# A fused attention and feed-forward kernel: the splits of the next v are placed in other slots of the seven-product tiles

## The chip, the cores and the metric

The kernel runs on one core of a Trainium2 chip. The metric is the device time of one execution, in microseconds (us), as the median of a few runs; three runs of the kernel before gave 2086.27, 2087.79 and 2088.13 us.

## The reference

Channel attention over 4 batches, and a feed-forward layer on its output, both in float32:

```python
def _attn_ref(q, k, v, tau):                       # q, k, v: (4, 6080, 256)
    qn = q / (np.linalg.norm(q, axis=1, keepdims=True) + 1e-06)
    kn = k / (np.linalg.norm(k, axis=1, keepdims=True) + 1e-06)
    s = kn.transpose(0, 2, 1) @ qn / tau           # 256 x 256 for each batch
    s = s - s.max(-1, keepdims=True)
    a = np.exp(s)
    a /= a.sum(-1, keepdims=True) + 1e-09
    return (v @ a).astype(np.float32)

def _moe_ref(x, w_in, w_out):                      # x: (24320, 256), w_in: (256, 2048), w_out: (2048, 256)
    h = x @ w_in
    g = np.maximum(0.01 * h, h)
    return (g @ w_out).astype(np.float32)
```

## The kernel before, in words

The kernel multiplies the attention matrix of a batch into `w_in`, so that a tile of v goes straight to h. A batch has 6 tiles of v, of twice 512 columns (the last two: twice 496), 24 tiles in all, counted here from 0 to 23. A tile is worked through in 8 **periods** (p0 to p7); each makes four 128-row blocks of h from seven block products (Strassen's scheme in Winograd's form: `block_product`, L1069, three matmuls each, since every operand is split into a high and a low half), applies the leaky unit, splits the result again and multiplies it with `w_out`.

In tiles 18 to 22 (`FAST`, the **seven-product tiles**) the product with `w_out` is also done with seven products instead of eight. They are called P1 to P7 (`fast_out`, L1206) and are issued one to four periods after the operand was made. A period of such a tile has 7 block products and 6 products with `w_out`: 13 times 3, so 39 matmuls. The seventh one, P4, of all 8 periods of a tile is put at the end of the next tile's p3 (`last_outs`): 24 matmuls, of which 13 are issued at the end of p3 and 11 in p4. So p3 has 52 matmuls and p4 has 50; these are the two long periods.

`fast_slot` (L1275) writes out one such period; each engine's instructions stand in the order in which it is called. TensorE's x and z are PSUM banks with one buffer each. In the order of VectorE (DVE) a period is:

- the middle slot, `slot("dve", ...)`, which takes work of the queue `dve` as long as its planned length (us) fits into the room given for this period;
- a slot for `dve_end`, then the low halves of C12 and C11 (`low`, L1167, the two `g_pair<-g_b`);
- the **first add** `add(i, h22, z)` (L1106): it reads bank z, and the block product "B22" that writes to z again (`block_product(i, p, z, S4, "B22", ...)`) waits for it;
- the low halves of T1 and T3, the second add `add(i, h12, z)`, the low halves of T2 and T4;
- a slot for `dve_end`, the low half of C22 (`g_pair<-g_a`), and in p3 and p4 a slot `dve` at the period's end.

The queue `dve` holds the work for the **next** tile's v. It is filled at given periods (`at(w + n, ...)`), where w is p0 of the tile. First come four maxima of v (`v_seen`, L158), then the gathering of the maximum over partitions (`gather` and `spread`, L163 to L177), the factors (`v_found`: L191 to L204 and L973), and 18 steps of `v_parts`: seven operands are split, each with a high half (`v_split_of`, L1012) and a low half (L1015), and four differences are made in place in `v_raw` (L1036). The tile `v_raw` has one buffer: the load of the v after the next (`v_load`, L996, two DMAs of 512 KB each on SyncE's queue) waits until the last split has read it. It is issued with p7 in the program:

```python
            at(w - (i in FAST) if i else 3, v_load, i + 1)
            elif i in FAST:
                at(w, v_scale_work, i + 1)
                for n in range(6):
                    at(w + 2 + n, v_go, i + 1, (3, 5, 5, 2, 2, 2)[n])
```

The queue `dve_end` takes the products P1 to P7 out of PSUM when a tile's last matmul of each was issued (`fast_end`): L1228 combines a bank and an earlier result, L1233 two results. The products with `w_out` of the last tile (23, with eight products, `ffn_out`, L1385) need the four banks `ps_o` that P1 to P4 of tile 22 leave.

On the POOL queue, each period issues four DMAs that add one g into another (`summed`, L1174); T1 to T4 are made from these sums.

Of the kernel before, what the change touches and what calls it, by code (L numbers as in the profile page):

```python
# [39 lines left out]
def channel_attention_ffn(  # L40
# [1095 lines left out]
    def p_has(g):  # L1136
        return g // NPAIR in FAST
# [137 lines left out]
    def fast_slot(i, p):  # L1275

        g = i * NPAIR + p
        n = widths[i % NT]
        seeded = not (p == 0 and widths[i % NT] > widths[(i - 1) % NT])
        w_split.pop((i, p - 1) if p else (i - 1, NPAIR - 1), None)  # L1280
        sums_start(g)
        order = ("P5", "P7", "P6", "P1", "P3") if p == 3 else ("P5", "P7", "P1", "P3", "P6")
        fast_outs(g, *order[:4 if p == 4 else 5])
        x, z = bank("x"), bank("z")
        block_product(i, p, x, A11, "B11", True, False)
        if seeded:
            run("act", lambda: nc.scalar.copy(out=z[:, 0:n], in_=x[:, 0:n]))
        else:
            h11 = taken(i, x)
        if g - 1 in fast_h:  # L1290
            run("act", unit, i - (p == 0), (p - 1) % NPAIR, "C12", fast_h.pop(g - 1), True)
        out(6)
        fast_do("act", high, g - 4, "T4")
        slot("dve", (3.0, 1.5, 2.3, 2.8, 2.8, 1.3, 1.3, 1.3)[p])
        block_product(i, p, z, A12, "B21", not seeded, True)
        block_product(i, p, x, S2, "T2", False, False)
        if not seeded:
            add(i, h11, z)
        run("act", unit, i, p, "C11", z if seeded else h11)
        h12 = taken(i, x)  # L1300
        out(4)
        slot("dve_end", 1.5)
        fast_do("act", high, g - 1, "C12")
        run("act", high, i, p, "C11")
        fast_do("act", high, g - 2, "T1")
        fast_do("dve", low, g - 1, "C12")
        run("dve", low, i, p, "C11")
        fast_outs(g, "P2", *(["P6"] if p == 4 else []))
        block_product(i, p, z, S1, "T1", True, False)
        block_product(i, p, x, S3, "T3", False, False)  # L1310
        h22 = taken(i, x)
        add(i, h22, z)
        out(6)
        fast_do("act", high, g - 2, "T3")
        fast_do("act", high, g - 3, "T2")
        slot("act_end", 0.65)
        fast_do("dve", low, g - 2, "T1")
        if p == 4:
            slot("dve_end", 0.8)
        fast_do("dve", low, g - 2, "T3")  # L1320
        if not p_has(g - 2):
            slot("dve", 1.5)
        block_product(i, p, x, A22, "T4", False, True)
        block_product(i, p, z, S4, "B22", False, True)
        run("act", unit, i, p, "C21", x, True)
        run("act", unit, i, p, "C22", h22)
        run("act", high, i, p, "C22")
        add(i, h12, z)
        fast_h[g] = h12
        last_outs(g)  # L1330
        out(15 if p == 3 else 24)
        if not p_has(g - 3):
            run("dve", low, i, p, "C22")
        fast_do("dve", low, g - 3, "T2")
        fast_do("dve", low, g - 4, "T4")
        slot("dve_end", 1.5)
        if p in (3, 4) or not p_has(g - 3):
            slot("dve", 1.3)
        if p_has(g - 3):
            run("dve", low, i, p, "C22")  # L1340

    def fast_rest(g):

# [80 lines left out]
    def slot(queue, room):  # L1424
        engine = queue.split("_")[0]
        while todo[queue] and todo[queue][0][0] <= room and todo[queue][0][1].ready():
            length, fn = todo[queue].popleft()
            room -= length
            with in_order(engine):
                ins = fn()  # L1430
            issued[engine] = ins
# [352 lines left out]
    for i in range(NTILES):  # L1784
        w = i * NPAIR
        if i + 1 < NTILES:
            at(w - (i in FAST) if i else 3, v_load, i + 1)
            if i + 1 < T16:
                at(w + (2 if i else 5), v_begin, i + 1)
                at(w + (4 if i else 6), v_work, i + 1, 2, 7)  # L1790
                at(w + 7, v_work, i + 1, 7, 11, i > 0)
            elif i in FAST:
                at(w, v_scale_work, i + 1)
                for n in range(6):
                    at(w + 2 + n, v_go, i + 1, (3, 5, 5, 2, 2, 2)[n])
            else:
                at(w + 1, v_scale_work, i + 1)
                at(w + 3, v_go, i + 1, 3)
                at(w + 4, v_go, i + 1, 3)
                at(w + 5, v_go, i + 1, 3)  # L1800
                at(w + 6, v_go, i + 1, 3)
        for p in range(NPAIR):
            if i:
                at(max(NPAIR - 2, w + p - 3), w_load, i, p)
# [233 lines left out]
    for i in range(NTILES):  # L2038
        for p in range(NPAIR):
            now[0] = i * NPAIR + p  # L2040
            for name in ("pe", "act"):
                todo[name].extend(todo[name + "_next"])
                todo[name + "_next"].clear()
            for fn, args in steps.get(i * NPAIR + p, ()):
                fn(*args)
            if i in FAST:
                assert (i // NT, p) in w_done 
                fast_slot(i, p)
                continue
            if i - 1 in FAST:  # L2050
                fast_rest(now[0])
            if p:
                w_split.pop((i, p - 1))
            x, y, z = bank("x"), bank("z" if i else "y"), bank("z")
            block_product(i, p, x, A11, "B11", True, False)
            h11 = taken(i, x)
            block_product(i, p, y, A12, "B21", True, True)
            slot("act", 0.65 if i else 0.75 if p else 1.5)
            slot("act_late", 0.65)
            add(i, h11, y)  # L2060
            if last is not None:
                leaky(i, p - 1, "C12", last)
                last = None
            slot("dve", 1.45 if i else 1.3)
            out(5)
            slot("pe", 1 if i and len(todo["pe"]) < 2 else 3)
            if i:
                leaky(i, p, "C11", h11)
            slot("dve", 2.2 if i else 2.6 if p < NPAIR - 1 else 1.5)
            if not todo["dve"]:  # L2070
                slot("dve_idle", 0.9)
            slot("act_end", 0.65)
            slot("dve_end", 1.5)
            assert (i // NT, p) in w_done
            block_product(i, p, x, S2, "T2", False, False)
            h12 = taken(i, x)
            if i == 0:
                leaky(i, p, "C11", h11)
                slot("dve", 1.0)
            if i:  # L2080
                slot("act", 1.8)
            block_product(i, p, z, S1, "T1", True, False)
            out(5)
            slot("pe", 1 if i or p else 2)
            block_product(i, p, x, S3, "T3", False, False)
            h22 = taken(i, x)
            add(i, h22, z)
            if i == 0:
                slot("act", 2.2)
            slot("dve", 1.45 if i else 2.8)  # L2090
            if not todo["dve"]:
                slot("dve_idle", 0.9)
            slot("act_end", 0.65)
            slot("dve_end", 1.5)
            out(8)
            slot("pe", 0 if i or p else 2)
            slot("pe_late", 1)
            if i == 0:
                slot("act", 0.6)
            else:  # L2100
                leaky(i, p, "C22", h22)
            block_product(i, p, x, A22, "T4", False, True)
            block_product(i, p, z, S4, "B22", False, True)
            add(i, h12, z)
            leaky(i, p, "C21", x)
            slot("act", 0.65 if i else 0.75)
            slot("act_late", 0.65)
            slot("dve", 0.8)
            if i == 0:
                leaky(i, p, "C22", h22)  # L2110
                slot("dve", 1.5)
            if i or p == NPAIR - 1:
                leaky(i, p, "C12", h12)
            else:
                last = h12
            out(24)
            last_outs(now[0])
            if i == NTILES - 1 and p < 4:
                outs.append(ffn_out(i, p, False))
                held.append(ffn_out(i, p, True))  # L2120
                if p == 3:
                    outs.extend(held)
                continue
            outs.append(ffn_out(i, p))
# [32 lines left out]
```

## Time and profile before

| | |
|---|---|
| median of three runs | 2087.79 us (2086.27 to 2088.13) |
| the profiled execution | 2087.2 us, its span 2085.2 us |
| TensorE (PE) busy | 2055.3 us, 99% of the span |
| VectorE (DVE) busy | 1691.6 us, 81% |
| ScalarE (ACT) busy | 1497.3 us, 72% |
| mean granted TensorE clock | 0.995 of full speed |
| tile 18, p0 to p7 | 1607.68 to 1675.03 us, 67.35 us |
| tile 19 | 1675.03 to 1747.93 us, 72.90 us |
| tile 20 | 1747.93 to 1828.97 us, 81.04 us |
| tile 21 | 1828.97 to 1908.48 us, 79.51 us |
| tile 22 | 1908.48 to 1987.50 us, 79.02 us |
| tile 23, to the end | 1987.50 to 2085.20 us, 97.70 us |

A period begins where TensorE starts its first matmul into bank x (`A11`); the times of the tiles are read from these. Times in all views are us from the span's start. In the timeline a row gives the start, the length, the engine, the line, the operation and its tiles; several like instructions in a row are one row (x2), and the idle time of the engine before the row stands in brackets with what ended it. An engine starts its next instruction before the one before has quite ended in these views, so the distance of two starts is what an instruction takes of the engine's time.

### The profile page before, as it was taken

The numbers are of one execution on the slowest core, as the hardware profiler recorded it, in microseconds if no ns is written. First come the engines' busy times: TensorE is split into PE (matmuls) and PEld (weight loads), VectorE is DVE, ScalarE is ACT, GpSimd is POOL, SyncE is SP. The second block draws the span as 40 slices with busy tenths as digits, with TensorE's granted clock in tenths as the row PEclk, the third lists the DMA queues.
The fourth block names the chain that finished last, engine by engine and source line by source line (L and its number), as shares of the span: only waits on it lengthen the run. The fifth ranks groups of instructions, "written<-read, shape, count | busy, mean of one in ns | idle before, by whom it ended". The sixth has DMA issues, their size and how long they took to land.

```text
span 2085.2 us, 27771 instructions
## 1 busy us (share of the span) xinstructions
PE 2055.3 (99%) x9516; PEld 1183.5 (57%) x9516; DVE 1691.6 (81%) x3112; ACT 1497.3 (72%) x2715; POOL 256.1 (12%) x331
## 2 busy tenths in 40 slices
PE   9999999999999999999999999999999999999998
PEld 8888888888865544544444444444444443434443
DVE  8988888878788878788888887877778897887873
ACT  6577777766578888877666666666666887877874
POOL 0000000000012232220001000000000343333310
PEclk9999999999999999999999999999999999999999
DMA  9946676655576997752333323332333776666630
GB/s 374 393 159 205 203 245 213 177 170 183 183 204 200 238 253 216 185 154 77 131 134 116 116 97 108 133 99 80 100 127 122 144 154 131 122 138 134 127 65 25
DMA packets 145438, 335.37 MB, mean 161 GB/s; under 512 B 18480, under 2 KB 38832, under 8 KB 145296
## 3 DMA queue, kind: packets, MB, share of 16 engines
q1 hardware_dynamic: 105776, 251.72, 36.0%
q0 software_dynamic: 39152, 81.55, 19.0%
q8 instruction: 75, 1.23, 0.3%
q14 instruction: 67, 0.55, 0.1%
q10 hardware_dynamic: 368, 0.32, 0.1%
HBM read 221.97 MB, written 57.42 MB: 134 GB/s over the span
## 4 chain that ended last, share of the span: by engine, by line
PE 91%; DVE 5%; ACT 2%; DMA 2%; issue 1%; SPq 0%; DVEq 0%; ACTq 0%
PE ps_o L1385 36%; PE ps_x L1069 22%; PE ps_z L1069 17%; PE ps_o L1206 5%; PE ps_s L336 4%; PE ps_o L336 2%; PE ps_y L336 2%; PE ps_s L1672 1%; PE ps_s L1206 1%; PE ps_y L1206 1%; DVE h L1106 1%; DVE g_pair L1167 1%; DMA v_raw<-in_vT_dram 1%; DVE v_split L1015 1%; ACT g L1089 0%
## 5 line engine op out<-in xcount | busy, mean ns | idle before, releaser
L1385 PE MATMUL ps_o<-g_split,w_out_split 128*128 128x512 f16 (+3 forms) x3456 | 846.5, 381 | 0.0
L1069 PE MATMUL ps_x<-v_split,w_split 128*128 128x512 f16 (+3 forms) x2280 | 621.7, 381 | 2.4 <-ACT h L1112 1.6
L1106 DVE TENSOR_TENSOR h<-ps_z,h 128x512 f32<-128x512 f32 (+1 forms) x529 | 360.6, 682 | 178.2 <-ACT h L1112 158.3
L1069 PEld LDWEIGHTS <-w_split 128*128 128x128 f16 x3024 | 293.7, 98 | 367.1 <-issue 34.7
L1099 DVE TENSOR_TENSOR g_split<-g,g_split 128x512 f16<-128x512 f32 (+3 forms) x576 | 393.6, 684 | 113.0 <-ACT g_split L1089 106.0
L1069 PE MATMUL ps_z<-v_split,w_split 128*128 128x512 f16 (+3 forms) x1704 | 463.5, 381 | 18.0 <-DVE h L1106 17.7
L1112 ACT COPY h<-ps_x 128x512 f32<-128x512 f32 (+1 forms) x537 | 309.3, 576 | 229.0 <-PE ps_x L1069 225.4
L1089 ACT ACTIVATE g<-h 128x512 f32<-128x512 f32 (+1 forms) x456 | 284.6, 624 | 202.9 <-DVE h L1106 200.4
L1385 PEld LDWEIGHTS <-w_out_split 128*128 128x128 f16 x2496 | 244.2, 98 | 291.6 <-issue 3.6
L1089 ACT ACTIVATE g_split<-h 128x512 f16<-128x512 f32 (+3 forms) x432 | 263.7, 610 | 0.0
L1385 PEld LDWEIGHTS ps_o<-g_split,w_out_split 128*128 128x128 f32 x1152 | 216.3, 188 | 43.5
L1069 PEld LDWEIGHTS ps_x<-v_split,w_split 128*128 128x128 f32 x576 | 107.7, 188 | 22.3 <-ACT g L1089 0.4
L1167 DVE TENSOR_TENSOR g_pair<-g_b,g_pair 128x512 f16<-128x512 f32 (+1 forms) x120 | 78.6, 682 | 32.2 <-ACT g_pair L1162 32.0
L1206 PE MATMUL ps_o<-g_pair,w_out_split 128*128 128x512 f16 (+1 forms) x360 | 100.5, 382 | 0.4 <-ACT g_pair L1162 0.3
L1015 DVE SCALAR_TENSOR_TENSOR v_split<-v_raw,v_scale,v_split 128x512 f16<-128x512 f32 (+1 forms) x125 | 93.0, 744 | 3.8
L1089 ACT ACTIVATE g<-ps_x 128x512 f32<-128x512 f32 (+1 forms) x152 | 89.5, 589 | 7.4 <-PE ps_x L1069 5.2
L1095 ACT CAST g_split<-g 128x512 f16<-128x512 f32 (+3 forms) x144 | 88.6, 615 | 4.6
L1069 PEld LDWEIGHTS ps_z<-v_split,w_split 128*128 128x128 f32 x408 | 76.2, 188 | 16.6 <-DVE h L1106 1.4
L1206 PEld LDWEIGHTS <-spare 128*128 128x128 f16 x480 | 47.6, 99 | 58.4 <-issue 4.2
L234 POOL MEMSET qk_raw<- 64x512 f32 x5 | 2.6, 521 | 585.2 <-ACT sq L260 267.6
L270 POOL DMA_DIRECT2D spare<-sq x48 | 43.9, 915 | 223.4 <-ACT sq L269 223.2
L1162 ACT CAST g_pair<-g_b 128x512 f16<-128x512 f32 (+1 forms) x120 | 69.7, 614 | 0.0
(263 smaller groups left out, 2353.0 us busy)
## 6 DMA issues: line engine op xcount, KB each, us to landing
w_split<-w_dram SPq DMA_DIRECT2D x104, 448.0 KB, 4.0
w_split<-w_dram SPq DMA_DIRECT2D x40, 896.0 KB, 5.0
qk_raw<-in_q_dram SPq DMA_DIRECT2D x115, 256.0 KB, 4.9
qk_raw<-in_k_dram SPq DMA_DIRECT2D x115, 256.0 KB, 5.1
v_raw<-in_vT_dram SPq DMA_DIRECT2D x32, 512.0 KB, 4.8
out_dram<-o_sb SPq DMA_DIRECT2D x64, 256.0 KB, 3.3
spare<-sq POOLq DMA_DIRECT2D x47, 256.0 KB, 5.3
g_a<-g_a POOLq DMA_DIRECT2D x32, 256.0 KB, 3.2
```

Of the source, the lines that this page charges most:

```text
L336: mm = nc.tensor.matmul(out=out, lhsT=lhsT, rhs=rhs, start=start, stop=stop, skip_group_check=True)
L1015: return nc.vector.scalar_tensor_tensor(out=sp[:, 1, 0:w], in0=src, scalar=up, in1=sp[:, 0, 0:w], op0=ALU.mult, op1=ALU.subtract)
L1069: mm = nc.tensor.matmul(out=ps[:, 0:n], lhsT=w[:, x, a, :], rhs=sp[:, y, 0:n], start=first and k == 0, stop=k == 2, skip_group_check=True,)
L1089: return nc.scalar.activation(out=to, in_=h[:, 0:n], func=AF.Prelu, alpha=0.01, scale=G_SCALE if i >= T16 else 1.0)
L1095: issued["act"] = nc.scalar.copy(out=sp[:, 0, 0:n], in_=out[:, 0:n])
L1099: issued["dve"] = nc.vector.tensor_tensor(out=sp[:, 1, 0:n], in0=out[:, 0:n], in1=f32(sp[:, 0, 0:n]), op=ALU.subtract)
L1106: issued["dve"] = nc.vector.tensor_tensor(out=h[:, 0:n], in0=ps[:, 0:n], in1=h[:, 0:n], op=ALU.add)
L1112: issued["act"] = nc.scalar.copy(out=h[:, 0:n], in_=ps[:, 0:n])
L1162: return nc.scalar.copy(out=sp[:, 0, 0:n], in_=g32[i, p, HELD.get(name, name)][:, 0:n])
L1167: return nc.vector.tensor_tensor(out=sp[:, 1, 0:n], in0=g32[i, p, HELD.get(name, name)][:, 0:n], in1=sp[:, 0, 0:n], op=ALU.subtract)
L1206: issued["pe"] = nc.tensor.matmul(out=ps[:, 0:n], lhsT=fast_lhsT(i, p, prod, x), rhs=sp[:, y, 0:n], start=p == 0 and k == 0, stop=p == NPA ...
L1385: issued["pe"] = nc.tensor.matmul(out=o_ps[i][j][h][:, 0:n], lhsT=wo_lhsT(i, x, f, h), rhs=sp[:, y, 0:n], start=p == 0 and early and k == ...
```

## The change

Four places. In `fast_slot` the rooms of the middle slot change for p1 (1.5 to 2.4), p3 and p4 (2.8 to 1.5). The `dve` slot at the period's end comes after the low half of C22 instead of ahead of it in p3 and p4, and has room 1.9 in p3 and in the first periods of tile 18, and 3.2 in p4. The steps of the next v are queued from p1 to p5 (1, 4, 6, 6, 2) instead of p2 to p7 (3, 5, 5, 2, 2, 2). In the last tile a slot of `dve_end` stands at the end of each period. The line numbers of the new file are one higher from L1332 on, and by up to three further down.

```diff
@@ -1291,7 +1291,7 @@
         fast_do("act", high, g - 4, "T4")
-        slot("dve", (3.0, 1.5, 2.3, 2.8, 2.8, 1.3, 1.3, 1.3)[p])
+        slot("dve", (3.0, 2.4, 2.3, 1.5, 1.5, 1.3, 1.3, 1.3)[p])
         block_product(i, p, z, A12, "B21", not seeded, True)
@@ -1329,15 +1329,16 @@
         out(15 if p == 3 else 24)
+        wide = p in (3, 4) or not p_has(g - 3)
         if not p_has(g - 3):
             run("dve", low, i, p, "C22")
         fast_do("dve", low, g - 3, "T2")
         fast_do("dve", low, g - 4, "T4")
         slot("dve_end", 1.5)
-        if p in (3, 4) or not p_has(g - 3):
-            slot("dve", 1.3)
         if p_has(g - 3):
             run("dve", low, i, p, "C22")
+        if wide:
+            slot("dve", 3.2 if p == 4 else 1.9)
@@ -1791,8 +1792,8 @@
                 at(w, v_scale_work, i + 1)
-                for n in range(6):
-                    at(w + 2 + n, v_go, i + 1, (3, 5, 5, 2, 2, 2)[n])
+                for n in range(5):
+                    at(w + 1 + n, v_go, i + 1, (1, 4, 6, 6, 2)[n])
@@ -2114,6 +2115,8 @@
             out(24)
+            if i == NTILES - 1:
+                slot("dve_end", 1.5)
             last_outs(now[0])
```

No instruction is added or dropped, and on PE, ACT, POOL and SP the instructions stand in the same order as before. Only DVE's order changes, in tiles 18 to 23. Three places of it:

DVE before, tile 19's last period and tile 20's first (in both, the two `g_pair<-g_b` are the low halves of C12 and C11, the row after them is the first add, and `v_split` and the maxima belong to the next tile's v):

```order
L1106 TENSOR_TENSOR h<-ps_z,h 128x512
L1167 TENSOR_TENSOR g_t<-g_b,g_t 128x512
L1167 TENSOR_TENSOR g_pair<-g_b,g_pair 128x512
L1167 TENSOR_TENSOR g_pair<-g_a,g_pair 128x512
L1015 SCALAR_TENSOR_TENSOR v_split<-v_raw,v_scale,v_split 128x512
L158 TENSOR_REDUCE v_scale<-v_raw 128x1 x3
L1167 TENSOR_TENSOR g_pair<-g_b,g_pair 128x512 x2
L1106 TENSOR_TENSOR h<-ps_z,h 128x512
```

DVE after the change, the same place:

```order
L1106 TENSOR_TENSOR h<-ps_z,h 128x512
L1167 TENSOR_TENSOR g_t<-g_b,g_t 128x512
L1167 TENSOR_TENSOR g_pair<-g_b,g_pair 128x512
L1167 TENSOR_TENSOR g_pair<-g_a,g_pair 128x512
L158 TENSOR_REDUCE v_scale<-v_raw 128x1 x4
L1167 TENSOR_TENSOR g_pair<-g_b,g_pair 128x512 x2
L1106 TENSOR_TENSOR h<-ps_z,h 128x512
```

The last low half of the split (T4's) stood right ahead of the maxima of the next load; now it stands in p6, two periods earlier, and four maxima instead of three stand in p0.

DVE after the change, from the end of tile 20's p0 to p1's first add (`o_sb` takes P3 and P2 of tile 19 out):

```order
L1167 TENSOR_TENSOR g_pair<-g_b,g_pair 128x512
L1228 SCALAR_TENSOR_TENSOR o_sb<-ps_o,v_scale,o_sb 128x512 x2
L1167 TENSOR_TENSOR g_pair<-g_a,g_pair 128x512
L163 TENSOR_REDUCE v_scale<-v_scale 128x1
...
L177 COPY zeros<-zeros 32x1 x3
L191 TENSOR_REDUCE v_scale<-zeros 32x1
...
L973 TENSOR_SCALAR v_scale<-v_scale,rest_down 128x1 x2
L1167 TENSOR_TENSOR g_pair<-g_b,g_pair 128x512 x2
L1106 TENSOR_TENSOR h<-ps_z,h 128x512
```

Before, one maximum (L158) stood there in place of the gathering and the factors, which came in p2 and p3. In tiles 19, 21 and 22 the rows of the change are the same.

DVE before and after, tile 23, end of p4 (the last `o_sb` of P4; `h<-ps_z` is p5's first):

```order
 L1106 TENSOR_TENSOR h<-ps_z,h 128x496
 L1099 TENSOR_TENSOR g_pair<-g,g_pair 128x496 x2
+L1228 SCALAR_TENSOR_TENSOR o_sb<-ps_o,v_scale,o_sb 128x496
 L1106 TENSOR_TENSOR h<-ps_z,h 128x496
 L1099 TENSOR_TENSOR g_pair<-g,g_pair 128x496
-L1228 SCALAR_TENSOR_TENSOR o_sb<-ps_o,v_scale,o_sb 128x496
 L1106 TENSOR_TENSOR h<-ps_z,h 128x496
```

It comes one add earlier. In the same way one of two `o_sb` rows of P3 and P2 moves ahead of an add at the end of tile 23's p0.

## Rows read from the trace of the kernel before

**Rows 1.** Waits of PE from 1600 us on: who waited for whom, us in total, times, longest.

```profile
PE ps_z L1069 <- DVE h L1106: 16.1, 7, 4.9
PE ps_o L1385 <- DVE o_sb L1228: 3.3, 1, 3.3
```

**Rows 2.** Stretches: us, busy of each engine (instructions), PEclk, DMA share, GB/s.

```profile
1675.03:1691.87 16.84, 16.84 (x80) 7.64 (x79) 16.06 (x32) 15.80 (x30) 6.93 (x8) 1.00 0.83 172
1747.93:1772.41 24.48, 19.61 (x79) 8.24 (x78) 15.71 (x26) 15.98 (x30) 7.07 (x9) 0.86 0.67 143
1760.31:1765.00 4.69, 4.69 (x12) 1.62 (x12) 4.36 (x8) 2.31 (x5) 0.00 (x0) 0.50 0.31 56
1828.97:1851.95 22.98, 18.60 (x80) 8.01 (x78) 16.11 (x27) 15.98 (x30) 6.22 (x8) 0.93 0.67 142
1908.48:1932.48 24.00, 19.40 (x79) 8.34 (x78) 16.00 (x27) 15.72 (x30) 7.79 (x9) 0.86 0.72 149
```

**Rows 3.** Timeline of DVE, the maxima of tile 20's p0 and of tile 19's p0.

```profile
1750.11 0.74 DVE L1015 SCALAR_TENSOR_TENSOR v_split<-v_raw,v_scale,v_split 128x512 f16<-128x512 f32 x1
1755.21 1.28 DVE L158 TENSOR_REDUCE v_scale<-v_raw 128x1 f32<-128x512 f32 x2 [4.36 <-DMA v_raw<-in_vT_dram]
1757.77 0.69 DVE L158 TENSOR_REDUCE v_scale<-v_raw 128x1 f32<-128x512 f32 x1 [1.28 <-DMA v_raw<-in_vT_dram]
...
1677.21 2.46 DVE L158 TENSOR_REDUCE v_scale<-v_raw 128x1 f32<-128x512 f32 x4
```

**Rows 4.** Timeline of SyncE's queue, the loads of v in tiles 18 and 20.

```profile
1670.08 0.85 SPq L996 DMA_DIRECT2D v_raw<-in_vT_dram  x2
...
1750.88 1.00 SPq L996 DMA_DIRECT2D v_raw<-in_vT_dram  x2
```

**Rows 5.** The long period p3 of tiles 19 and 20, as stretches.

```profile
1700.28:1711.89 11.61, 11.39 (x54) 5.09 (x52) 11.57 (x20) 8.66 (x16) 4.65 (x5) 1.00 0.74 133
1780.83:1792.92 12.09, 11.38 (x53) 5.06 (x52) 11.86 (x28) 8.77 (x16) 3.49 (x4) 1.00 0.64 116
```

**Rows 6.** Timeline of PE: the "B22" product into z in tile 19's p7 and p3.

```profile
1746.85 0.81 PE L1069 MATMUL ps_z<-v_split,w_split 128*128 128x512 f16 x3
...
1708.01 0.81 PE L1069 MATMUL ps_z<-v_split,w_split 128*128 128x512 f16 x3 [0.22 <-DVE h L1106]
```

**Rows 7.** Timeline of DVE in tile 19's p3: a split's high and low half, the first low halves.

```profile
1703.12 0.52 DVE L1012 TENSOR_SCALAR v_split<-v_raw,v_scale 128x512 f16<-128x512 f32 x1
...
1704.35 0.48 DVE L1012 TENSOR_SCALAR v_split<-v_raw,v_scale 128x512 f16<-128x512 f32 x1
1704.75 1.40 DVE L1228 SCALAR_TENSOR_TENSOR o_sb<-ps_o,v_scale,o_sb 128x512 f32<-128x512 f32 x2
1706.07 1.28 DVE L1167 TENSOR_TENSOR g_pair<-g_b,g_pair 128x512 f16<-128x512 f32 x2
```

**Rows 8.** Timeline of DVE in tile 19's p1 and p2: begin and end of gathering and factors.

```profile
1686.94 0.15 DVE L163 TENSOR_REDUCE v_scale<-v_scale 128x1 f32<-128x4 f32 x1
...
1688.30 1.29 DVE L1167 TENSOR_TENSOR g_pair<-g_b,g_pair 128x512 f16<-128x512 f32 x2
...
1694.05 0.14 DVE L191 TENSOR_REDUCE v_scale<-zeros 32x1 f32<-32x4 f32 x1
...
1695.59 0.52 DVE L1012 TENSOR_SCALAR v_split<-v_raw,v_scale 128x512 f16<-128x512 f32 x1
```

**Rows 9.** Timeline of DVE in tile 19's p5, the first low halves.

```profile
1727.25 1.29 DVE L1167 TENSOR_TENSOR g_pair<-g_b,g_pair 128x512 f16<-128x512 f32 x2 [2.10 <-ACT g_pair L1162]
```

**Rows 10.** Timeline of DVE in tile 23, p5's first add.

```profile
2040.61 0.68 DVE L1106 TENSOR_TENSOR h<-ps_z,h 128x496 f32<-128x496 f32 x1 [3.69 <-PE ps_z L1069]
```

**Rows 11.** Timeline of POOL's queue: sums in tile 19's p3, and beside tile 18's load.

```profile
1703.38 1.54 POOL L1174 DMA_DIRECT2D g_b<-g_a  x1
1706.33 0.86 POOL L1174 DMA_DIRECT2D g_a<-g_b  x1 [1.41 <-DMA g_a<-g_a]
...
1677.98 0.86 POOL L1174 DMA_DIRECT2D g_b<-g_b  x1 [3.75 <-DMA g_b<-g_a]
```

## The prediction, made before the result

> **What bounds the kernel now.** TensorE is busy 99% of the span, so the question is where it stands still, and I read its waits first. From 1600 us on two of them matter [rows 1]: bank z waits for VectorE's add, 16.1 us in 7 waits, the longest 4.9, and `ps_o` in the last tile waits once, 3.3 us, for VectorE to take a product out. Both lie in the tiles that the change touches. The reader should see that ACT and the loads do not stand in these rows themselves: TensorE waits for an add, and the add stands behind something on VectorE.
>
> What it stands behind, the timeline of VectorE shows [rows 3]. In tile 20's p0 the low half of the last split runs at 1750.11, and then VectorE, which works in order, is idle for 4.36 us until the new v has landed, and for 1.28 more until its second half has. SyncE could issue the load only at 1750.88 [rows 4], right after that split had read the one buffer. In tile 18 the load went out at 1670.08, and the four maxima of tile 19's p0 then run from 1677.21 without idle time [rows 3, 4].
>
> The stretches give the price [rows 2]. Two undisturbed periods (tile 19's p0 and p1) take 16.84 us, 8.42 each. The same two take 24.48 in tile 20, 22.98 in tile 21, 24.00 in tile 22. More is lost than the wait itself, because the granted clock is 0.50 (1.2 GHz) in the 4.69 us after TensorE restarts at 1760.31 [rows 2].
>
> **The change part by part.**
>
> *The splits end in p6.* T4's low half moves from the next tile's p0 to p6's middle slot, which begins about 2.2 us into a period (the maxima of tile 19 start at 1677.21, 2.18 after 1675.03 [rows 2, 3]). High and low half take 1.2 us, so the load goes out about 3.5 us into p6, some 16 us before the maxima of the next p0 begin. In tile 20 the last half of v was there 6.9 us after the issue (1757.77 against 1750.88 [rows 3, 4]), so 9 us are to spare, and the two DMAs queue ahead of nothing that TensorE needs: SyncE's stores of the tile's products come in p0 to p4. The loss in p0 and p1 goes: 7.64 + 6.14 + 7.16 = **20.9 us** (tile 22's second period is a little shorter by itself, so its part is rather low). The clock's part goes with the wait.
>
> *The middle slot of p3 is smaller.* Today the first low halves start at 1706.07 in tile 19's p3 [rows 7] and the product into z starts at 1708.01 [rows 6], 1.94 later. Undisturbed, as in p7, it starts at 1746.85, 7.34 after its period's begin (1747.93 less 8.42) [rows 2, 6]. So there is a rule to count with: the delay of a period is the start of the first low halves within it, plus 1.94, less 7.34. Tile 19's p3 gives 5.79 + 1.94 - 7.34 = 0.39. The stretch agrees: 11.61 against 52 matmuls at 8.42/39, 11.23, so 0.38 [rows 2, 5]. In tile 20 the same period takes 12.09, 0.86 too much [rows 5], and tiles 21 and 22 have the same order of work. After the change this slot holds one low and one high half, 1.2 us, instead of two of each in tile 19 and the factors with one of each in the others. Two products of 0.66 are taken out behind it as today, so the first low halves start near 2.18 + 1.2 + 1.3 = 4.7, under the 5.4 at which a delay begins. Gain: 0.38 + 3 x 0.86 = **3.0 us**.
>
> *Gathering and factors come together in p1.* This is the new wait. In tile 19's p1 the gathering begins at 1686.94 [rows 8], behind two products taken out and the low half of C22. That is 3.49 after the period's begin (1675.03 + 8.42). It takes 1.36 (to 1688.30), the factors 1.54 (1694.05 to 1695.59) [rows 8]. Together the first low halves start at 3.49 + 2.90 = 6.39, and the rule gives 6.39 + 1.94 - 7.34 = 1.0 us. The order is the same in tiles 19 to 22: **cost 4.0 us**. Queued behind it are the two low halves, the first add, and then TensorE. Such a short stop leaves the clock alone: it is 1.00 in tile 20's p3 [rows 5]. p2 begins 0.2 us late on VectorE, with work for 2.4, and stays under 5.4. The ends of the price: 0, if the idle time that VectorE has before the adds were larger than the rule says, and 1.5 each, if the small operations wait on each other more than in these rows.
>
> *The ends of p3 and p4.* p3's end and p4's middle now hold a low half and the four differences less one; TensorE has 13 matmuls more than usual there, 2.8 us, and the first low halves of p4 wait for ACT anyway. p4's end and p5's middle hold one difference, three high and three low halves, against one difference, two high and one low today. One pair takes 1.23 (1703.12 to 1704.35 [rows 7]), so 1.9 us are added; today VectorE is idle 2.10 us there, waiting for ACT [rows 9]. Nothing is lost: 0.2 us of idle time and the 0.8 between ACT's end and the limit remain. If this cover is missing, each 0.1 us too much costs 0.1 us, four times.
>
> *Tile 18* has no long periods, since no P4 products come before it, yet p4's end has the room of 3.2. Four high and three low halves stand between C22's low half (its end at 2.18) and p5's first low halves: 3 x 1.23 + 0.40 (1704.35 to 1704.75 [rows 7]) = 4.1, start 6.27, delay **0.9 us**. The other moves in tile 18's p0 to p3 shift one maximum and the gathering; ACT holds TensorE there, and I take 0 within 0.4 either way.
>
> *The last tile.* Taking P4 out comes one add earlier. Today VectorE is idle for 3.69 us just ahead of that add [rows 10], long enough for the 0.7 us that it takes, while TensorE reaches the bank later. The wait of 3.3 us [rows 1] goes: **3.3 us**. At the end of p0 another product moves ahead of p1's first add, one such operation, 0.66 (1704.75 to 1706.07 for two [rows 7]). I take all of it as a cost, **0.7 us**; the other end is 0.
>
> Sum: 20.9 + 3.0 + 3.3 - 4.0 - 0.9 - 0.7 = 21.6 us. The profiled execution took 2087.2, so 2065.6; the median of the runs lies 0.6 above it, so **2066.2 us**.
>
> *A rule that speaks against the change.* In p3 to p5 VectorE works in one piece, and POOL must issue its sums beside it. The rows show that today: in tile 19's p3 VectorE is busy 11.57 of 11.61 us [rows 5], and POOL issues its sums at 1703.38 and 1706.33 [rows 11], the second after waiting for the sum before and not for VectorE. The Trainium skill, page "SBUF — State Buffer", section "SBUF: two separate sides", says that descriptors of a DMA from the POOL queue are written by GpSimd, which is locked out of a port that it shares with VectorE while certain VectorE operations run, so that the DMA looks blocked by VectorE. By that rule longer unbroken runs would hold the sums; the trace shows at most an issue of 1.54 us instead of 0.86. The sum stays with the rows; by the rule it would be that of rival 4.
>
> **The rivals.**
> 1. *The new stops cost nothing.* Then the three costs fall away: 2066.2 - 5.6 = 2060.6 us. For it speaks only that PE's ends are modelled; against it, that the rule gave tile 19's p3 within 0.02. Chance 0.08.
> 2. *The ends of the long periods are too full.* If ACT's casts do not leave the idle time that I count on, both p4's and p5's first adds come late, up to 0.75 us each in four tiles: 6 us, 2072 us. Against it: 2.10 us idle [rows 9]. Chance 0.13.
> 3. *The load is not what p0 waits for,* or does not go out earlier because something else holds SyncE. Then only p3 and the last tile gain, and the costs stay: 2087.8 - 6.3 + 5.6 = 2087.1, no change. Against it: tile 18 to 19, where an early load let the maxima run [rows 3, 4]. Chance 0.05.
> 4. *Slower: POOL's sums come late.* The load now runs beside the sums of p6 and p7, and VectorE's longer runs may hold their issue. Beside tile 18's load one sum was issued 3.75 us late [rows 11], and tile 19's p0 still took 8.42 [rows 2], so such a delay is free. Held for the 9 us of a whole run, a sum would make T3 and so TensorE wait 9 - 3.75 = 5.2 us in each of 8 long periods: +42, 2108 us. It outweighs the gain from 2.7 us in each, that is from 6.5 us of delay. Chance 0.04. This is what the rule of the Trainium skill's page above would do at its worst.
>
> **How the numbers follow.** The forecast keeps 0.70. The range goes from rival 1's time to rival 2's, 2060.5 to 2072, and leaves out rivals 3 and 4 and the tails of the forecast. What a measurement of this kernel can tell from no change is about 0.2%, 4.2 us; faster by more are the forecast and rivals 1 and 2: 0.91; the same is rival 3: 0.05; slower is rival 4: 0.04.
>
> **What would show it.** Right: the maxima of tiles 20 to 22 start without waiting for the load; p0 takes 8.4 us in each; p1 takes about 9.4 in tiles 19 to 22 with z waiting 0.8 or so for the add; p3 takes 11.2; the wait for `o_sb` is gone. Wrong: a wait for `v_raw` on VectorE in p0, a granted clock of 0.50 in tiles 19 to 22, p4 or p5 longer than 10.8 and 8.4, or POOL's sums as what T1 or T3 waits for.

## The result, and the profile after

The changed kernel took 2065.24 us (median of five runs, 2064.48 to 2066.83), the kernel before 2087.79 in the same comparison (2086.27 to 2089.53). The ratio is 0.9893, interval 0.9879 to 0.9907: faster by 22.6 us, or 1.1%. The prediction was 2066.2 us.

The waits of PE from 1600 us on, in the changed kernel (who waited for whom, us in total, times, longest), answer to [rows 1]:

```profile
PE ps_z L1069 <- DVE h L1106: 4.6, 6, 0.8
PE ps_x L1069 <- ACT h L1112: 0.8, 2, 0.4
```

Bank z waited 16.1 us, now 4.6, and the longest wait is 0.8 instead of 4.9. The wait for `o_sb` in the last tile is gone. What is left of bank z's waits are six short stops: four in p1 of tiles 19 to 22, one in tile 18's p5, one in tile 23's p1.

The stretches of the changed kernel (us, busy of each engine, PEclk, DMA share, GB/s): p0 and p1 of tiles 19, 20, 21 and 22, which answer to [rows 2], then p3 of tiles 19 and 20, which answer to [rows 5], and tile 23's p5:

```profile
1675.76:1693.59 17.83, 16.99 (x79) 7.63 (x78) 17.00 (x42) 16.57 (x31) 8.09 (x10) 1.00 0.76 145
1749.28:1767.12 17.84, 17.00 (x79) 7.63 (x78) 17.01 (x42) 16.57 (x31) 7.32 (x9) 1.00 0.73 140
1822.82:1840.65 17.83, 16.99 (x79) 7.62 (x78) 17.00 (x42) 16.57 (x31) 6.90 (x8) 1.00 0.69 133
1896.34:1913.80 17.46, 16.66 (x80) 7.64 (x79) 16.66 (x40) 16.31 (x31) 7.39 (x9) 1.00 0.70 135
1702.01:1713.24 11.23, 11.23 (x53) 5.05 (x52) 10.51 (x18) 8.65 (x16) 4.25 (x5) 1.00 0.70 126
1775.54:1786.77 11.23, 11.23 (x53) 5.07 (x52) 10.51 (x18) 8.66 (x16) 3.59 (x5) 1.00 0.63 112
2020.29:2033.47 13.18, 13.18 (x64) 6.17 (x63) 4.54 (x7) 6.09 (x11) 0.00 (x0) 1.00 0.01 2
```

The first four are now alike: in tiles 20 to 22, 24.48, 22.98 and 24.00 us have become 17.84, 17.83 and 17.46, and tile 19, which had 16.84, lost 1 us. The clock is 1.00 in all of them. In p3 TensorE is busy for all of the 11.23 us.

The timeline of SyncE's queue, tile 19's p6 (begins at 1732.45), and that of VectorE in tile 20's p0 answer to [rows 4] and [rows 3]:

```profile
1735.92 0.84 SPq L996 DMA_DIRECT2D v_raw<-in_vT_dram  x2
```

```profile
1750.86 0.68 DVE L1167 TENSOR_TENSOR g_pair<-g_a,g_pair 128x512 f16<-128x512 f32 x1
1751.46 2.45 DVE L158 TENSOR_REDUCE v_scale<-v_raw 128x1 f32<-128x512 f32 x4
1753.86 1.29 DVE L1167 TENSOR_TENSOR g_pair<-g_b,g_pair 128x512 f16<-128x512 f32 x2
```

The load goes out 3.47 us into p6 and 15.5 us ahead of the first maximum. The four maxima run in one piece, with no idle time in brackets: VectorE no longer waits for the load.

The new stop stands in p1. VectorE in tile 19's p1 (begins at 1684.17), and what PE did:

```profile
1687.67 0.15 DVE L163 TENSOR_REDUCE v_scale<-v_scale 128x1 f32<-128x4 f32 x1
...
1690.33 0.34 DVE L973 TENSOR_SCALAR v_scale<-v_scale,rest_down 128x1 f32<-128x1 f32 x2
1690.58 1.28 DVE L1167 TENSOR_TENSOR g_pair<-g_b,g_pair 128x512 f16<-128x512 f32 x2
1691.78 0.68 DVE L1106 TENSOR_TENSOR h<-ps_z,h 128x512 f32<-128x512 f32 x1
```

```profile
1692.52 0.81 PE L1069 MATMUL ps_z<-v_split,w_split 128*128 128x512 f16 x3 [0.84 <-DVE h L1106]
```

Gathering and factors take 2.91 us (1687.67 to 1690.58), so the first low halves start 6.41 after the period's begin, and bank z waits 0.84 for the add behind them. The period takes 9.42 us instead of 8.42.

One number of the profiled execution needs a word. It was the slowest of the five, 2066.83, and its last store landed late. The timeline of ACT's queue shows that store, first in the changed kernel and then before:

```profile
2059.78 0.35 ACTq L1413 DMA_DIRECT2D out_dram<-o_sb  x1
```

```profile
2082.07 0.35 ACTq L1412 DMA_DIRECT2D out_dram<-o_sb  x1
```

From there to the span's end are 5.1 us, against 3.2 before and 3.2 in each of the six experiments below. TensorE's last group of matmuls ended at 2058.74 instead of 2081.03 (start and length of the last row of its timeline, 2052.30 + 6.44 and 2074.59 + 6.44), which is 22.3 us earlier. This number I compare with the steps below.

### The profile page after: what moved, and what is told of

The parts are those of the page before. It is cut to its first block, busy times and chain, and to the rows that moved or that the text cites. A ratio compares the mean times of both kernels' runs of the same rounds, so it can differ in the third digit from the quotient of the medians.

```text
span 2064.9 us, 27776 instructions
## 1 busy us (share of the span) xinstructions
PE 2048.8 (99%) x9516; PEld 1182.9 (57%) x9516; DVE 1691.7 (82%) x3112; ACT 1496.6 (72%) x2715; POOL 256.2 (12%) x331
## 4 chain that ended last, share of the span: by engine, by line
PE 93%; DVE 4%; ACT 2%; issue 1%; DMA 0%; DVEq 0%; ACTq 0%
PE ps_o L1386 37%; PE ps_x L1069 22%; PE ps_z L1069 17%; PE ps_o L1206 5%; PE ps_s L336 4%; PE ps_o L336 2%; PE ps_y L336 2%; PE ps_s L1673 1%; PE ps_y L1206 1%; PE ps_s L1206 1%; DVE h L1106 1%; DVE g_pair L1167 1%; ACT g L1089 0%; DVE g_split L1099 0%; PE ps_y L740 0%
```

## The experiments

In each, the instructions of PE, ACT and POOL stand in the same order as in the changed kernel; only VectorE's order differs (in late_t4 SyncE also issues one load of weights ahead of three stores, in tile 18's p0). Nothing of the computation is left out. The diffs are against the changed kernel, but for the second, which is against the one before. The kernel before stood at 2087.4 us beside the first four and at 2087.78 beside the last two. Lengths of periods are distances between starts of `A11`.

**The splits without the last tile's slot (splits_only).**

```diff
-            if i == NTILES - 1:
-                slot("dve_end", 1.5)
```

> The change without the new slot in the last tile. My theory (the two parts are separate): the last tile's wait for the bank comes back (its p5 16.7 us instead of 13.2) and its p1 gets 0.65 us back (11.2 instead of 11.84), so 2065.2 + 3.5 - 0.65 = 2068.1 us; tiles 18 to 22 as in the change, 73.9 us for tiles 19 to 21. Rival (the earlier splits also free the last tile, so the new slot is not needed): 2064.6 us, p5 at 13.2.

Measured: 2069.57 us (2069.1 to 2071.78), ratio 0.9919, 0.9906 to 0.9933. Tiles 18 to 22 have the lengths of the changed kernel within 0.02 us; the wait of 3.34 us for `o_sb` in tile 23's p5 is back. That p5 took 18.37 us, 1.69 more than before, although its stop is the same. Stretch of p5, here and then in the kernel before, and PE behind the stop here:

```profile
2019.14:2037.51 18.37, 15.03 (x65) 6.56 (x64) 5.19 (x8) 6.20 (x11) 0.00 (x0) 0.91 0.04 15
```

```profile
2039.08:2055.76 16.68, 13.34 (x64) 6.16 (x63) 5.19 (x8) 6.20 (x11) 0.00 (x0) 1.00 0.04 16
```

```profile
2023.90 1.21 PE L1386 MATMUL ps_o<-g_pair,w_out_split 128*128 128x496 f16 x5 [3.34 <-DVE o_sb L1228]
2024.94 1.40 PE L1069 MATMUL ps_x<-v_split,w_split 128*128 128x496 f16 x3
...
2028.93 0.79 PE L1069 MATMUL ps_x<-v_split,w_split 128*128 128x496 f16 x3
```

Three matmuls took 1.40 us about a microsecond after the restart and 0.79 later: here the clock fell after the stop, a price that the expected 2068.1 us did not have. So the splits alone carry most of the gain, 17.8 of 22.6 us by the medians, and the last tile's slot can be worth more than its wait.

**The last tile's slot alone (last_tile_only).**

```diff
+            if i == NTILES - 1:
+                slot("dve_end", 1.5)
```

> The kernel before with only the new slot in the last tile. My theory: minus 3.5 us (no wait for the bank in p5) plus 0.65 us (p1's first add is later), 2087.8 - 2.85 = 2084.9 us; tile 20 still 81.0 us. Rival (taking P4 out earlier only moves the wait to the next add): 2087.8 us or a little more, with p6 or p5 longer.

Measured: 2083.91 us (2082.36 to 2085.81), ratio 0.9986, 0.9977 to 0.9995. Stretches of tile 20's p0 and p1, and of tile 23's p5:

```profile
1748.31:1773.06 24.75, 19.70 (x79) 8.22 (x78) 15.71 (x26) 15.97 (x30) 7.07 (x9) 0.86 0.67 142
...
2041.02:2054.20 13.18, 13.18 (x64) 6.16 (x63) 4.54 (x7) 6.08 (x11) 0.00 (x0) 1.00 0.01 2
```

The last tile's p5 is that of the changed kernel, 13.18 us; p1 takes 11.84 instead of 11.20, as there. The wait for the load in tiles 20 to 22 is still there. By the medians this half is worth 3.5 us alone and 4.3 on top of the splits (2069.57 less 2065.24). The two halves sit in different tiles, and 17.8 and 3.5 add up to 21.3 of the 22.6 us. That the slot is worth more on top of the splits fits the clock's fall in splits_only, though only one execution of it was profiled.

**T4's split stays in the next tile's p0 (late_t4).** All else of the change is kept; the room of p0 is raised so that both halves and the maxima fit.

```diff
-        slot("dve", (3.0, 2.4, 2.3, 1.5, 1.5, 1.3, 1.3, 1.3)[p])
+        slot("dve", (4.3, 2.4, 2.3, 1.5, 1.5, 1.3, 1.3, 1.3)[p])
...
-                for n in range(5):
-                    at(w + 1 + n, v_go, i + 1, (1, 4, 6, 6, 2)[n])
+                for n in range(4):
+                    at(w + 1 + n, v_go, i + 1, (1, 4, 6, 6)[n])
+                at(w + NPAIR, v_go, i + 1, 2)
```

> The change, but T4's split stands in the next tile's p0 again, ahead of the four maxima; all else keeps its place. My theory (p0 waits for the load, and the load for this split): in p0 of tiles 19 to 22 the load goes out 3.5 us into the period, its halves land 4.3 and 6.9 us later, the first low halves start near 11.7 instead of 4.6, so p0 gets 11.7 + 1.94 - 7.34 = 6.3 us longer and the granted clock falls after it, some 2.9 us more as before: 4 x 9.2 = 37 us, 2102 us, slower than the kernel before. Rival (VectorE's amount of work in p0 is what counts, the load is not): 1.2 us more work in p0, first low halves at 5.8, 0.4 us in each of four tiles, 2066.8 us.

Measured: 2098.73 us (2097.45 to 2100.79), ratio 1.0058, 1.0044 to 1.0072: slower than the kernel before. Tile 19's p0 in the timelines of SyncE's queue and of VectorE, and p0 and p1 as a stretch:

```profile
1679.72 0.85 SPq L996 DMA_DIRECT2D v_raw<-in_vT_dram  x2
```

```profile
1678.94 0.75 DVE L1015 SCALAR_TENSOR_TENSOR v_split<-v_raw,v_scale,v_split 128x512 f16<-128x512 f32 x1
1684.57 1.28 DVE L158 TENSOR_REDUCE v_scale<-v_raw 128x1 f32<-128x512 f32 x2 [4.87 <-DMA v_raw<-in_vT_dram]
```

```profile
1676.24:1702.27 26.03, 19.46 (x79) 8.17 (x78) 18.63 (x44) 15.98 (x30) 7.36 (x9) 0.87 0.62 134
```

One step, put back, brings back the loss: the load goes out right behind it, the maxima wait, and z waits 6.57 us (6.26, 6.77 and 7.44 in tiles 20 to 22). p0 and p1 of the four tiles lose 8.2, 8.1, 8.5 and 8.9 us against the changed kernel, 33.7 together; the medians differ by 33.5. That is more than the kernel before lost, since tile 19 now waits too; there its load had gone out in tile 18's p7 [rows 4]. So it is this step and its load that p0 waited for. Two things I had not foreseen. The larger room also takes work into tile 18's p0, which grows by 1.7 us (11.88 against 10.21). And I had added 9.2 us to each pair of the changed kernel: against an undisturbed pair of 16.84 tile 19's does lose 9.2, but the changed kernel's pair has a stop of 1.0 of its own in p1, and here no wait for the add stands in p1. That is most of the 3.3 us by which the time lies under the 2102 us expected.

**A longer middle slot in p1 (fuller_p1).** The first operand's split, a high and a low half, goes into p1 as well.

```diff
-        slot("dve", (3.0, 2.4, 2.3, 1.5, 1.5, 1.3, 1.3, 1.3)[p])
+        slot("dve", (3.0, 3.7 if i > FAST[0] else 2.4, 2.3, 1.5, 1.5, 1.3, 1.3, 1.3)[p])
...
-                    at(w + 1 + n, v_go, i + 1, (1, 4, 6, 6, 2)[n])
+                    at(w + 1 + n, v_go, i + 1, ((3, 2, 6, 6, 2) if i > FAST[0] else (1, 4, 6, 6, 2))[n])
```

> The change with one high and one low half more in p1's middle slot of tiles 19 to 22 (taken from p2 and p3). My theory (a period's delay is the start of its first low halves plus 1.94 less 7.34): the start goes from 6.39 to 7.6, p1 gets 1.2 us longer in four tiles, 10.6 us instead of 9.42 and TensorE's stop 2.0 us instead of 0.84, the clock stays at 1.00: 2065.2 + 4.8 = 2070.0 us. Rivals: the longer stop lowers the clock, some 2.5 us more in each, 2080 us; or p1's stop comes from the chain of small operations alone and not from the sum of the work, then no change, 2065.2 us.

Measured: 2070.6 us (2069.3 to 2071.74), ratio 0.992, 0.9905 to 0.9935. Stretches: p1 and p2 of tile 19, p1 of tile 20, and PE's restart in each:

```profile
1684.40:1695.97 11.57, 9.54 (x40) 4.01 (x39) 10.86 (x32) 8.77 (x16) 4.31 (x5) 0.92 0.74 147
1695.97:1705.12 9.15, 9.15 (x41) 4.02 (x40) 7.11 (x13) 7.18 (x14) 3.45 (x4) 0.92 0.50 90
1760.81:1771.42 10.61, 8.58 (x41) 3.82 (x40) 10.18 (x31) 8.58 (x16) 4.27 (x5) 1.00 0.76 151
```

```profile
1693.93 1.39 PE L1069 MATMUL ps_z<-v_split,w_split 128*128 128x512 f16 x3 [2.03 <-DVE h L1106]
...
1770.34 0.81 PE L1069 MATMUL ps_z<-v_split,w_split 128*128 128x512 f16 x3 [2.03 <-DVE h L1106]
```

In tile 20 the stop grows from 0.84 to 2.03: 1.19 for a pair of 1.2 us, one for one, as the rule of the prediction counts. Tiles 21 and 22 are alike (2.00, 1.96). In tile 19 the same stop of 2.03 us took the clock down as well: three matmuls took 1.39 us behind it, and p1 and p2 together 20.7 instead of 17.8. Why there and not in the others stays open. The profiled execution is the slowest of the four, so the median need not hold this fall.

**The factors back in p2 (factors_in_p2).** p1 has the room of the kernel before, so the factors come in p2; p3's end takes the step that this displaces.

```diff
-        slot("dve", (3.0, 2.4, 2.3, 1.5, 1.5, 1.3, 1.3, 1.3)[p])
+        slot("dve", (3.0, 1.5, 2.3, 1.5, 1.5, 1.3, 1.3, 1.3)[p])
...
-            slot("dve", 3.2 if p == 4 else 1.9)
+            slot("dve", 3.2 if p == 4 else 2.7 if p == 3 and i > FAST[0] else 1.9)
```

> The change with the factors in p2 again (p1's middle slot 1.5 instead of 2.4) and the room at p3's end 2.7 instead of 1.9 in tiles 19 to 22, so that the splits still end in p6. My theory (p1's stop comes from gathering and factors standing together): p1 8.42 us in tiles 19 to 21 instead of 9.42, p2, p3 and p4 without loss (the first low halves start at 4.8, 4.7 and 4.8 after the period's begin, under 5.4): 4.0 us less, 2061.2 us. Rival (VectorE has too much work in p0 to p3 wherever it stands): the stop moves on to p2 or p4, 2064 to 2066 us.

Measured: 2060.93 us (2060.8 to 2061.03), ratio 0.9869, 0.9855 to 0.9884. PE's waits from 1600 us on, and tile 20's p0 and p1:

```profile
PE ps_z L1069 <- DVE h L1106: 1.3, 2, 0.7
```

```profile
1748.15:1764.98 16.83, 16.83 (x79) 7.64 (x78) 16.05 (x32) 15.79 (x30) 6.91 (x8) 1.00 0.74 141
```

The four stops are gone and none came up elsewhere; TensorE runs through p0 and p1. It is 4.3 us faster than the changed kernel, so those stops were a price that the change need not have paid.

**All three costs taken out (all_three).** As the one before; tile 18's ends also have the room of 1.9, and the last tile's slot leaves out p0.

```diff
-            slot("dve", 3.2 if p == 4 else 2.7 if p == 3 and i > FAST[0] else 1.9)
+            slot("dve", 1.9 if i == FAST[0] else 3.2 if p == 4 else 2.7)
...
-            if i == NTILES - 1:
+            if i == NTILES - 1 and p:
```

> As factors_in_p2, and also: the room at the ends of tile 18's p3 and p4 is 1.9 (its p5 loses its stop, 0.75 us), and the last tile's new slot stands from p1 on (its p1 gets 0.65 us back, 11.2 us). My theory: 2061.2 - 0.75 - 0.65 = 2059.8 us. Rival (tile 18's T4 now ends in p7, the load goes out too late for tile 19's p0): tile 19's p0 waits for the load, 2 us or more back.

Measured: 2059.35 us (2059.02 to 2060.02), ratio 0.9863, 0.9847 to 0.9879. All waits of PE from 1600 us on that come to 0.7 us or more:

```profile
PE ps_x L1069 <- ACT h L1112: 0.8, 2, 0.4
PE ps_x L1069 <- ACT g L1089: 0.7, 1, 0.7
```

Bank z waits for no add any more. Tile 18's p5 is 8.42 again, tile 23's p1 11.20, and tile 19's p0 stays at 8.42. This version beats both kernels: by 28.4 us the one before, by 5.9 the changed one (the kernel before stood at 2087.79 beside the changed one and at 2087.78 beside this).

Not tried: a second buffer for `v_raw`.

## Why the prediction was right, step by step

The mechanism held, and each term was near its size. Two starts on VectorE were counted wrong, in p3 and in p5, and neither cost anything. Expected against measured (lengths of the same periods in the two profiled executions; gains positive):

| step | expected | measured |
|---|---|---|
| The splits end in p6 | +20.9 | +21.3 |
| The middle slot of p3 is smaller | +3.0 | +2.8 |
| Gathering and factors come together in p1 | -4.0 | -4.0 |
| The ends of p3 and p4 | 0 | 0 |
| Tile 18 (p5; p0 to p3) | -0.9; 0 | -0.75; -0.1 |
| The last tile: wait gone | +3.3 | +3.5 |
| The last tile: p1's add later | -0.7 | -0.6 |
| sum | +21.6 | +22.2 |

The measured sum accounts for the 22.3 us by which TensorE ended earlier; 0.1 lies ahead of tile 18.

*The splits end in p6.* p0 and p1 of tiles 20 to 22 lost 6.64, 5.15 and 6.54 us with the new stops of 1.00, 1.00 and 0.96 in them, so 21.3 without. What lies above the forecast is tile 22, whose undisturbed pair is 16.50 and not 16.84, as the prediction allowed for. That so large a term came out this close is in part luck: in last_tile_only, with the order of the kernel before in these tiles, the same pairs took 24.75, 23.01 and 24.61 us, 0.9 more in all. late_t4 shows the cause: undo that one step, and the load, the wait and the slow stretch are back. Rival 3 (the load is not what p0 waits for) falls with it.

*The rule for delays* (start of the first low halves, plus 1.94, less 7.34) was the best tool. Tile 19's p1: 6.41 + 1.94 - 7.34 = 1.01, measured 1.00. Tile 18's p5, where the low halves start at 1655.90 in a period that begins at 1649.76: 6.14 + 1.94 - 7.34 = 0.74, measured 0.75. fuller_p1 adds 1.2 and gets 1.19. Rival 1 (the new stops cost nothing) falls: factors_in_p2 gives the 4 us back.

*The middle slot of p3* gave its gain. No run undoes this part alone; what speaks for it is that the rule prices the period before as well. VectorE before, tile 20's p3 (begins at 1780.83 [rows 5]):

```profile
1787.11 1.28 DVE L1167 TENSOR_TENSOR g_pair<-g_b,g_pair 128x512 f16<-128x512 f32 x2
```

6.28 + 1.94 - 7.34 = 0.88, and this period took 0.86 too much. But one detail of the step was wrong. After the change the low halves were to start near 4.7; they start at 5.41. VectorE in the changed kernel, tile 19's p3 (begins at 1702.01):

```profile
1706.10 1.41 DVE L1228 SCALAR_TENSOR_TENSOR o_sb<-ps_o,v_scale,o_sb 128x512 f32<-128x512 f32 x2 [0.72 <-PE ps_o L1206]
1707.42 1.28 DVE L1167 TENSOR_TENSOR g_pair<-g_b,g_pair 128x512 f16<-128x512 f32 x2
```

The product that is taken out there is not ready earlier: VectorE waits 0.72 us for TensorE's matmuls. I had counted VectorE's work alone. The start stands just at the limit of 5.4, so nothing was lost; that the 0.7 which I had missed just fitted was luck.

*The ends of p3 and p4* cost nothing, but with less room than I gave them. Tile 19's p5 (begins at 1724.03):

```profile
1723.96 0.69 DVE L1167 TENSOR_TENSOR g_pair<-g_a,g_pair 128x512 f16<-128x512 f32 x1 [0.16 <-ACT g_pair L1162]
...
1728.15 0.75 DVE L1015 SCALAR_TENSOR_TENSOR v_split<-v_raw,v_scale,v_split 128x512 f16<-128x512 f32 x1
1728.82 1.29 DVE L1167 TENSOR_TENSOR g_pair<-g_b,g_pair 128x512 f16<-128x512 f32 x2
```

The low halves start at 4.79 with no idle time ahead of them, where 0.2 was to be left; ACT no longer ends the wait, VectorE's own work does. Some of that is a wait that the new order brought: the low half of C22, now ahead of the slot, waits 0.16 for ACT. 0.6 us of room remain to the limit. p4 takes 10.79 and p5 8.42, so rival 2 (ends too full) did not come. No run puts these ends back alone.

*The last tile.* The add ahead of which P4 is now taken out comes after 3.04 us of idle time, where it had 3.69 [rows 10]:

```profile
2018.05 0.73 DVE L1228 SCALAR_TENSOR_TENSOR o_sb<-ps_o,v_scale,o_sb 128x496 f32<-128x496 f32 x1
2021.82 0.67 DVE L1106 TENSOR_TENSOR h<-ps_z,h 128x496 f32<-128x496 f32 x1 [3.04 <-PE ps_z L1069]
```

The operation runs in VectorE's idle time, as counted. The term was 0.2 too small: a period grows by 0.16 more than the wait that the view gives (0.84 and 1.00 in tile 19's p1, 3.34 and 3.50 here). It is too small by more where the clock falls after the stop, as in splits_only: there p5 is 5.2 us longer than in the changed kernel.

*Rival 4 (POOL's sums late).* In tile 19's p4 and p5 VectorE works in one piece from 1723.96 on. That stretch, and POOL's queue in it:

```profile
1723.96:1733.00 9.04, 9.04 (x44) 4.12 (x42) 8.71 (x15) 7.38 (x14) 3.79 (x4) 1.00 0.65 118
```

```profile
1725.48 1.54 POOL L1174 DMA_DIRECT2D g_b<-g_a  x1
1728.47 0.86 POOL L1174 DMA_DIRECT2D g_a<-g_b  x1 [1.45 <-DMA g_a<-g_a]
```

VectorE is busy 8.71 of 9.04 us, and POOL issues four sums in that time, the longest in 1.54 us; the 0.86 of the next came after a wait for a sum, not for VectorE. TensorE does not stop here.

The Trainium skill, page "SBUF — State Buffer", section "SBUF: two separate sides", says that GpSimd, which writes the descriptors of the POOL queue's DMAs, can be locked out of a port while certain VectorE operations run. The trace does not show TensorE held up by it: no issue of a sum takes over 1.54 us, and before the change the longest took 1.55 (1.54 in [rows 11]). Whether VectorE's operations here are of that kind, and whether the 0.68 above the usual 0.86 is that lock, no run shows.

## What to carry to other kernels

When one buffer is loaded again for the next tile, what counts is when its last reader runs, not how long the load takes: look for the last small step that reads it, and move that step ahead by more than the load's latency. For an engine that works in order, note from one undisturbed period the latest start at which the next engine is not held; a few starts read from the trace then price a late start to a few hundredths of a microsecond here. The start itself is harder to foresee: it was 0.7 us off in p3, where VectorE had to wait for another engine. When freed work is put somewhere else, fill the slots only to that limit: the same change without its three overfull slots was another 5.9 us faster.

## What the runs showed of the hardware that was not expected

The length of a stop does not by itself tell whether the clock falls. Stops of 0.84 us never lowered it (1.00 in the stretches shown above), and those of 4.4 to 4.9 in the kernel before were followed by slow matmuls each time. Between them it went both ways: 2.03 us in tile 19 of fuller_p1 lowered it, 2.03, 2.00 and 1.96 in the next three tiles did not; 3.34 us in tile 23 lowered it in splits_only and not in the kernel before, where the stretch behind the same stop had a clock of 1.00. What else decides was not tried.

The last store, of the same size and from the same engine, took 3.2 us to the span's end in seven of the eight profiled executions and 5.1 in one. What made that one late is not shown.
